# First batch's attention in plain float32 matmuls instead of split float32r operands

## The chip, the cores and the metric

One Trainium2 chip, one core. The metric is the device time of one launch in microseconds (us). The kernel before takes 722.84 us, the median of 3 runs (721.26 to 723.34).

## The reference, cut to what matters

```python
def _attn_ref(q, k, v, M_prev, z_prev, beta):        # B, H, S, D = 4, 8, 576, 64
    scores = (1 / sqrt(D)) * q @ k^T                  # per batch and head, causal
    a = exp(scores - max); a /= a.sum(-1) + 1e-9
    local = a @ v
    q_p = phi(q)                                      # phi(x) = x + 1 if x > 0, else exp(x)
    mem_out = (q_p @ M_prev) / (q_p . z_prev + 1e-6)
    g = 1 / (1 + exp(-beta))                          # per head
    return g * mem_out + (1 - g) * local

def reference(...):
    x = attn_out.transpose(0, 2, 1, 3).reshape(B * S, H * D)     # 2304 x 512
    r = maximum(x @ w_in, 0)                                     # 2304 x 2048
    return (s * r * r + b) @ w_out                               # 2304 x 512
```

All inputs but `w_in` and `w_out` are float32; these two come in as 64-bit floats and are converted on the chip.

## The kernel before, in words

TensorE multiplies float32r operands in one pass, and float32r keeps fewer bits than float32. So the kernel writes a float32 operand as two float32r parts, H (the rounded value) and L (the value less H), and sums the products H·H, H·L and L·H.

The work goes by pairs of heads: pair g holds heads x = 2g and 2g + 1, a batch has NP = 4 pairs, and the first batch is pairs 0 to 3, heads 0 to 7. There are 32 heads. For each of them:

- `load_qk` (L158) loads q and k of a pair, transposed (128 partitions, 64 for each head). `split_qk` (L214) makes parts in the tile `sqk`: H of both by one ACT copy (L223), L of q on one of DVE and POOL and L of k on the other (L220). `stack_qk` (L241) copies these parts by two DMAs a head into `X` (L251), so that one contraction over 128 partitions holds two of the three products.
- `s_mm` (L273) makes the scores of a query tile into PSUM by two matmuls (L278, L279), at least 192 columns wide; the causal tiles have 64, 192, 448, 320 and twice 288 columns. `s_red` (L292, DVE) adds the mask and finds the row's extreme, `s_exp` (L300, ACT) makes P, `s_norm` (L312) scales it on POOL, one tile of the five on DVE.
- `pt_bank` (L335) transposes P block by block on TensorE (L342) into one of five PSUM banks `tps`, and `evac` takes a bank out: ACT writes H (L209), DVE writes L (L213). k block 0 goes to `pt`, the others to `pth` and `ptl`.
- phi(q) is made by ACT, DVE and POOL (L189 to L205), transposed (`t_phi`, L237), taken out as H and L by `evac`, and stacked by two DMAs a head into `Q` (`stack_qp`, L260). `split_v` makes H of M_prev and V on ACT (L269) and L on POOL (L270).
- `av_mm` (L364) sums phi(q)·M and P·V in one PSUM bank `ops`, once for query columns 320 to 575 ("hi", 10 matmuls) and once for columns 0 to 319 ("lo", 6 matmuls), lines L371 to L375; `av_evac` adds the two halves of the output's partitions (ACT copy L387, DVE add L388). There is one bank `ops`, so the next sum waits until the bank is taken out.
- `x_split` makes H and L of the pair's attention output on POOL (L399, L400).

Beside it `split_w` converts w_in in 16 pieces (`conv64`, ACT L78, DVE L79 to L81, POOL L418 and L419). `mm1` (L430 to L432) multiplies the attention output by w_in; its first matmul needs all four pairs of the first batch. `mm1` of batch b runs in between the attention of batch b + 1. From L540 on stands the second stage, the product with w_out, which the change does not touch.

What sets the order: the table `T` at the top gives each task of a head a position (head number plus an offset); the tasks are issued in order of position, and a scheduler in the compiler then orders each engine's instructions by its own model of them. Every engine, and the DMA queue of SP too, works its list in order. The program is one long list without loops.

Of the kernel before, what the change touches and what calls it, by code (L numbers as in the profile page):

```python
# [8 lines left out]
F32 = mybir.dt.float32  # L9
# [18 lines left out]
def attention_moe_kernel(  # L28
# [15 lines left out]
    nc = tc.nc  # L44
# [54 lines left out]
    PTS = []  # L99
    for i in range(2):  # L100
        PTS.append((
            ap1.tile([128, S], F32R, name=f"pt0_{i}"),
            ap1.tile([128, 6, 256], F32R, name=f"pth_{i}"),
            ap1.tile([128, 6, 256], F32R, name=f"ptl_{i}"),
        ))
# [223 lines left out]
    ]}  # L329
    ROW = {(1, 3): 0, (2, 3): 1, (3, 3): 2, (1, 1): 3, (1, 4): 0, (2, 4): 1, (3, 4): 2, (4, 4): 5, (1, 2): 3, (2, 2): 4}  # L330

    def pt_bank(x, blocks):
        P = st["P", x]
        pt0, pth, ptl = PTS[x % 2]
        ps = ps_t.tile([128, 512], F32, tag="t", name="tps")  # L335
        o = 0
        runs = []
        for j, i in blocks:
            kn = 128 if j else 64
            qn = 128 if i else 64  # L340
# [160 lines left out]
    def at(t, fn, *a):  # L501
        EV.append((t, len(EV), fn, a))
# [7 lines left out]
    for n, job in enumerate(JOBS):  # L510
        if job is None:
            continue
        k = len(job[1])
        for i in range(3):
            at(2 * n + TKP[k][i], split_qk, n, i)
        at(2 * n + LQK[k], load_qk, n)
        at(2 * n + LQK[k] + 0.01, load_z, n)
        at(2 * n + LV[k], load_v, n)
# [3 lines left out]
            at(2 * n + PHI[4 + c], t_phi, n, c)  # L522
        for j in range(2):
            x = 2 * n + j
            at(x + SXP[k], stack_qk, x)
            a = [(0,), (1,), (2,), (3,), (4, 0, 288), (4, 288, 288)]
            for pos, a in zip(SP[k], a if k == 5 else a[:3] if k == 3 else a[3:]):
                at(x + pos, t_score, x, *a)
            at(x + SQP[k], stack_qp, x)
            at(x + SPV[k], split_v, x)  # L530
            for pos, bl in zip(PTP[k], PTB[k]):
                at(x + pos, pt_bank, x, bl)
            for c in range(2):
                if CT[c][0] in job[1]:
                    at(x + AVP[k][1 - c], t_av, x, c)
# [268 lines left out]
```

## Time and profile before, and how to read it

| | us |
|---|---|
| median of 3 runs | 722.84 |
| the profiled execution's own time | 729.97 |
| span of that execution, first to last instruction | 727.2 |
| PE busy, share of the span | 630.5, 87% |
| DVE busy | 515.3, 71% |
| ACT busy | 475.2, 65% |
| POOL busy | 459.1, 63% |
| mean granted clock of TensorE | 0.943 |

PE is TensorE's matmuls, PEld its weight loads, DVE the vector engine, ACT the scalar engine, POOL GpSimd, SP the engine that issues the DMAs. Busy time of PE holds the overlapped ends of pipelined matmuls, so what a matmul costs in a row of others is the distance from one start to the next. The granted clock is a mean over a stretch in which the clock stands at one of two levels, 2.4 GHz (1.00) or 1.2 GHz (0.50). The first batch's attention fills about the first 140 us.

### The profile page before, as it was taken

How to read it: one execution, taken by the hardware profiler on the slowest of the kernel's cores; microseconds unless marked ns; L12 is line 12 of the kernel's file. 1: busy time of each engine (PE TensorE's matmuls, PEld its weight loads, DVE VectorE, ACT ScalarE, POOL GpSimd, SP SyncE). 2: the span in 40 equal slices, each digit the busy share in tenths (PEclk: the TensorE clock that was granted, in tenths of full speed). 3: DMA queues.
4: the chain of work that ended last, by engine and by line, in shares of the span. 5: the costliest groups of instructions: out<-in, count | busy, mean ns of one | idle time of the engine just before them, and what ended most of it. 6: DMA issues, size and time to landing. Idle time of an engine off the chain costs nothing. (4 is left out here: it accounts for less than half of the span.)

```text
span 727.2 us, 13086 instructions
## 1 busy us (share of the span) xinstructions
PE 630.5 (87%) x4504; PEld 595.3 (82%) x4504; DVE 515.3 (71%) x1099; ACT 475.2 (65%) x1062; POOL 459.1 (63%) x454
## 2 busy tenths in 40 slices
PE   0667676889889899999999999967869999999997
PEld 0456555789778899999999899967859999999997
DVE  2767798786777766775675753499977867776774
ACT  2556577547667576776776664448878877777851
POOL 4648669756586554655574622488987776565683
PEclk9989988689999899999999999988979999999999
DMA  7968856848788566867786632748355353353301
GB/s 196 280 166 202 208 141 171 208 121 214 182 210 229 149 160 176 218 161 208 207 215 159 161 103 82 265 149 280 134 159 145 117 145 118 115 145 112 102 21 58
DMA packets 73858, 119.87 MB, mean 165 GB/s; under 512 B 10048, under 2 KB 48960, under 8 KB 73792
## 3 DMA queue, kind: packets, MB, share of 16 engines
q1 hardware_dynamic: 73792, 119.04, 59.8%
q8 instruction: 35, 0.57, 0.3%
q14 instruction: 31, 0.25, 0.1%
HBM read 57.68 MB, written 23.59 MB: 112 GB/s over the span
## 5 line engine op out<-in xcount | busy, mean ns | idle before, releaser
L300 ACT ACTIVATE P<-P,mn 128x64 f32<-128x64 f32 (+4 forms) x160 | 89.6, 562 | 42.5 <-DVE mn L292 42.1
L671 PE MATMUL yps<-bH,op 128*128 128x256 f32 x360 | 103.1, 288 | 7.6 <-POOL op L661 6.2
L312 POOL TENSOR_SCALAR P<-P,sm,omg 128x64 f32<-128x64 f32 (+3 forms) x128 | 86.2, 687 | 33.8 <-DVE sm L308 16.3
L669 PE MATMUL yps<-bH,op 128*128 128x256 f32 x360 | 102.9, 286 | 2.4 <-ACT op L660 2.2
L278 PE MATMUL sps<-X 128*128 128x192 f32 (+2 forms) x192 | 69.6, 364 | 40.1 <-DMA X<-sqk 20.7
L670 PE MATMUL yps<-bL,op 128*128 128x256 f32 x360 | 102.5, 285 | 0.0
L342 PE MATMUL tps<-ident,P 128*128 128x128 f32 (+2 forms) x480 | 83.0, 293 | 13.2 <-POOL P L312 5.0
L430 PE MATMUL hps<-xs,w1H 128*128 128x320 f32 (+1 forms) x256 | 80.9, 316 | 10.9 <-ACT r L439 7.8
L430 PE MATMUL hps<-xs,w0H 128*128 128x320 f32 (+1 forms) x256 | 79.0, 312 | 8.1 <-ACT r L439 7.7
L292 DVE CUSTOM_DVE_ANT_0 P<-sps,mask 128x64 f32<-128x64 f32 (+4 forms) x160 | 65.5, 424 | 28.2 <-PE sps L279 24.5
L278 PEld LDWEIGHTS sps<-X 128*128 128x128 f32 x192 | 40.2, 209 | 48.8 <-DVE mn L292 26.0
L342 PEld LDWEIGHTS tps<-ident,P 128*128 128x128 f32 (+2 forms) x480 | 60.4, 142 | 23.4 <-issue 10.4
L431 PE MATMUL hps<-xs,w1H 128*128 128x320 f32 (+1 forms) x256 | 78.3, 306 | 0.0
L432 PE MATMUL hps<-xs,w1L 128*128 128x320 f32 (+1 forms) x256 | 77.6, 305 | 0.0
L671 PEld LDWEIGHTS yps<-bH,op 128*128 128x128 f32 x360 | 69.1, 192 | 9.7 <-POOL op L661 6.4
L432 PE MATMUL hps<-xs,w0L 128*128 128x320 f32 (+1 forms) x256 | 76.9, 302 | 0.0
L431 PE MATMUL hps<-xs,w0H 128*128 128x320 f32 (+1 forms) x256 | 76.8, 301 | 0.0
L669 PEld LDWEIGHTS yps<-bH,op 128*128 128x128 f32 x360 | 69.4, 193 | 3.0 <-ACT op L660 3.0
L439 ACT ACTIVATE r<-hps 128x320 f32<-128x320 f32 (+1 forms) x128 | 49.5, 407 | 31.9 <-PE hps L432 24.7
L670 PEld LDWEIGHTS yps<-bL,op 128*128 128x128 f32 x360 | 69.4, 193 | 0.0
L213 DVE TENSOR_TENSOR ptl<-tps,pth 128x512 fp32r<-128x512 f32 (+1 forms) x96 | 56.5, 595 | 16.6 <-ACT pth L209 10.7
L279 PE MATMUL sps<-X 128*128 128x192 f32 (+2 forms) x192 | 62.4, 327 | 0.0
(119 smaller groups left out, 2052.4 us busy)
## 6 DMA issues: line engine op xcount, KB each, us to landing
X<-sqk SPq DMA_DIRECT2D x64, 432.0 KB, 5.7
r_d<-r SPq DMA_DIRECT2D x32, 320.0 KB, 4.3
qks<-in_qk_t_dram SPq DMA_DIRECT2D x16, 576.0 KB, 5.2
Q<-sqp SPq DMA_DIRECT2D x64, 144.0 KB, 4.5
xa<-in_moe_w_in_dram SPq DMA_DIRECT2D x16, 512.0 KB, 6.4
r_d<-r SPq DMA_DIRECT2D x32, 256.0 KB, 4.3
raw<-in_moe_w_out_dram SPq DMA_DIRECT2D x16, 512.0 KB, 5.6
w1L<-r_d SPq DMA_DIRECT2D x16, 512.0 KB, 4.6
```

Of the source, the lines that this page charges most:

```text
L278: nc.tensor.matmul(ps[:, :m], lhsT=lhsT, rhs=X[:, 1, c0:c0 + m], start=True, stop=False)
L279: nc.tensor.matmul(ps[:, :m], lhsT=lhsT, rhs=X[:, 2, c0:c0 + m], start=False, stop=True)
L292: nc.vector.tensor_tensor_reduce(P[:, PO[i] + c0:PO[i] + c0 + n], ps[:, :n], mask[:, mo:mo + n], -SCALE, init, ALU.add, ALU.min, mn[:, o:o ...
L300: nc.scalar.activation(pt, pt, AF.Exp, scale=-1.0, bias=mn[:, o:o + 1], accum_out=sm[:, i:i + 1])
L312: dve("nm", x // 2, i).tensor_scalar(pt, pt, sm[:, i:i + 1], omg[:, h:h + 1], ALU.mult, ALU.mult)
L342: nc.tensor.transpose(ps[0:kn, o:o + qn], P[0:qn, c:c + kn], ident[0:qn, 0:qn])
L430: nc.tensor.matmul(ps, lhsT=wH[:, p, fs], rhs=xs[:, 0], start=p == 0, stop=False)
L431: nc.tensor.matmul(ps, lhsT=wH[:, p, fs], rhs=xs[:, 1], start=False, stop=False)
L432: nc.tensor.matmul(ps, lhsT=wL[:, p, fs], rhs=xs[:, 0], start=False, stop=p == NP - 1)
L669: nc.tensor.matmul(ps, lhsT=H, rhs=BH, start=f == 0, stop=False)
L670: nc.tensor.matmul(ps, lhsT=H, rhs=BL, start=False, stop=False)
L671: nc.tensor.matmul(ps, lhsT=L, rhs=BH, start=False, stop=f == KF - 1)
```

## The change

For heads 0 to 7 q, k, phi(q), M, V and P^T stay float32, and TensorE gets them as float32. q and k are loaded straight into their place (`sqk` for pairs 0 and 1, the memory of `X` for pairs 2 and 3), M and V into `V`; `split_qk`, `stack_qk`, `stack_qp` and `split_v` are not issued for these pairs. A score tile is one matmul over a head's 64 partitions, without the minimum of 192 columns. `t_phi` and `pt_bank` take a bank out by one ACT copy. `av_mm32` makes 64 output partitions by 6 ("hi") and 4 ("lo") matmuls, leaving out columns whose P is zero, and one DVE copy takes them out. The fills of `pth` and `ptl` with zeros move from the start to heads 8 and 9. Pairs 4 to 15 and the table `T` are as before.

```diff
+    def new_pts(i, dtype):
+        PTS[i] = pts = tuple(ap1.tile(s, dtype, tag=f"{n}_{i}", name=f"{n}_{i}")
+                             for n, s in (("pt0", [128, S]), ("pth", [128, 6, 256]), ("ptl", [128, 6, 256])))
+        if dtype == F32R:
+            for t in pts[1:]:
+                nc.gpsimd.memset(t[:, 4:6, 0:128].bitcast(F32), 0.0)
...
@@ load_qk
-        st["qk", g] = t = ap1.tile([128, 2, S], F32, tag="qks", name="qks")
+        if g < NP:
+            if g < 2:
+                t = qk[:, 2 * g:2 * g + 2].bitcast(F32)
+            else:
+                t = ap1.tile([128, 2, S], F32, tag=f"X{g % 2}", name="qk32")
...
@@ load_v
+        if g < NP:
+            st["V", 2 * g] = st["V", 2 * g + 1] = t = ap2.tile([128, 6, 2, D], F32, tag="V", name="V32")
...
@@ t_phi
+        if g < NP:
+            nc.scalar.copy(s[:, cs], ps[:, :o])
+        else:
+            evac(s[:, 0, cs], s[:, 1, cs], ps[:, :o], ("phl", g, c))
...
@@ s_mm
+        if x < 2 * NP:
+            t = st["qk", x // 2][64 * (x % 2):64 * (x % 2) + 64]
+            nc.tensor.matmul(ps[:, :n], lhsT=t[:, 0, QS[i]:QS[i] + 128], rhs=t[:, 1, c0:c0 + n], start=True, stop=True)
+            return ps
...
+    def pt_evac(x, H_out, L_out, ps, key):
+        if x < 2 * NP:
+            nc.scalar.copy(H_out, ps)
+        else:
+            evac(H_out, L_out, ps, key)
...
+    def av_mm32(x, hi):
+        g, j = divmod(x, 2)
+        V, Q = st["V", x], st["sqp", g]
+        pt0, pth, _ = PTS[j]
+        ps = ps_o.tile([128, 512], F32, tag="o", name="ops")
+        q0, n = CO[hi], CW[hi]
+        rs = slice(64 * j, 64 * j + 64)
+        off = 0 if hi else 64
+        nc.tensor.matmul(ps[0:64, :n], lhsT=V[rs, 0, j], rhs=Q[rs, q0:q0 + n], start=True, stop=False)
+        nc.tensor.matmul(ps[0:64, :n], lhsT=V[rs, 1, j], rhs=pt0[rs, q0:q0 + n], start=False, stop=False)
+        for r, c, o in ((0, 2, 0), (1, 3, 0), (2, 4, 0), (5, 5, 128)) if hi else ((3, 2, 0), (4, 3, 128)):
+            nc.tensor.matmul(ps[0:64, off + o:n], lhsT=V[:, c, j], rhs=pth[:, r, o:], start=False, stop=r in (4, 5))
+        return ps
...
@@ av_evac
+        if x < 2 * NP:
+            nc.vector.tensor_copy(xo[ma, :], ps[0:64, :n])
+            return
...
@@ the list of tasks
+        own = n >= NP
         for i in range(3):
-            at(2 * n + TKP[k][i], split_qk, n, i)
+            if own:
+                at(2 * n + TKP[k][i], split_qk, n, i)
...
-            at(x + SXP[k], stack_qk, x)
+            if own:
+                at(x + SXP[k], stack_qk, x)
...
-            at(x + SQP[k], stack_qp, x)
-            at(x + SPV[k], split_v, x)
+            if own:
+                at(x + SQP[k], stack_qp, x)
+                at(x + SPV[k], split_v, x)
```

How the order moves, at three places. First the DMA queue of SP at the start. Before, from its sixth entry on (`qks` are q and k of a pair, `X_146` and `X_174` the stacks of heads 0 and 1, `xa` pieces of w_in):

```order
L177 DMA qs<-in_q_rows_dram 128x640
L183 DMA vs<-in_vm_dram 128x768
L251 DMA X_146<-sqk 64x1728
L163 DMA qks<-in_qk_t_dram 128x1152
L251 DMA X_146<-sqk 64x3x576
L251 DMA X_174<-sqk 64x3x576
L251 DMA X_174<-sqk 64x1728
L183 DMA vs<-in_vm_dram 128x768
L171 DMA z<-in_z_prev_dram 128x128
L406 DMA xa<-in_moe_w_in_dram 128x1024 x3
```

Now, from the same entry:

```order
L183 DMA qs<-in_q_rows_dram 128x640
L169 DMA sqk<-in_qk_t_dram 128x1152
L192 DMA V_152<-in_vm_dram 128x768
L169 DMA qk_194<-in_qk_t_dram 128x1152
L192 DMA V_284<-in_vm_dram 128x768
L169 DMA qk_375<-in_qk_t_dram 128x1152
L169 DMA qks<-in_qk_t_dram 128x1152
L192 DMA vs<-in_vm_dram 128x768
L177 DMA z<-in_z_prev_dram 128x128
L455 DMA xa<-in_moe_w_in_dram 128x1024 x3
```

The stacks are gone; the loads of pairs 1 to 4 stand ahead of the first pieces of w_in.

Second, DVE about head 1's way out (a row that only reads an accumulator is shown once). Before (`x_398` is pair 0's output, `pth` and `ptl` the parts of P^T, here of head 2):

```order
L388 TENSOR_TENSOR x_398<-ops,xc 64x320
L312 TENSOR_SCALAR P<-P,sm,omg 128x320
L213 TENSOR_TENSOR ptl_104<-tps,pth_103 128x4x128 x2
L213 TENSOR_TENSOR ptl_104<-tps,pth_103 128x2x128
L213 TENSOR_TENSOR pt_0_102<-tps,pt_0_102 64x64
L292 ISA P,mn<-sps,mask 128x64
L292 ISA mn 128x1
L292 ISA P,mn<-sps,mask 128x192
L220 TENSOR_TENSOR sqk<-qks,sqk 128x576
L213 TENSOR_TENSOR pt_0_102<-tps,pt_0_102 64x512
L292 ISA P,mn<-sps,mask 128x448
```

Now (`x_326` is pair 0's output):

```order
L432 COPY x_326<-ops 64x320
L311 ISA P,mn<-sps,mask 128x448
L311 ISA mn 128x1
L311 ISA P,mn<-sps,mask 128x320
L311 ISA P,mn<-sps,mask 128x288
L229 TENSOR_TENSOR sqk<-qks,sqk 128x576
L311 ISA P,mn<-sps,mask,mn 128x288
L311 ISA P,mn<-sps,mask 128x64
L311 ISA P,mn<-sps,mask 128x192
L326 TENSOR_SCALAR sm<-sm 128x5
L327 RECIPROCAL sm<-sm 128x5
```

The subtractions for the parts L are gone; reductions of scores follow each other. The one `sqk` entry that is left belongs to pair 4.

Third, PE about the "hi" sum of head 4. Before (`X_850` is the stack of head 7, `pth_103` and `ptl_104` the parts of P^T of head 4):

```order
L372 MATMUL ops<-pt_0_102,V 128x256
L374 MATMUL ops<-pth_103,V 128x256
L375 MATMUL ops<-ptl_104,V 128x256
L278 MATMUL sps<-X_850 128x192
L279 MATMUL sps<-X_850 128x192
L278 MATMUL sps<-X_850 128x448
L279 MATMUL sps<-X_850 128x448
```

Now (`qk_375` is q and k of pair 3 in float32, here for head 6, `V_472` M and V of pair 2):

```order
L292 MATMUL sps<-qk_375 128x320
L403 MATMUL ops<-pt_0_229,V_472 64x256
L405 MATMUL ops<-pth_230,V_472 64x256 x3
L405 MATMUL ops<-pth_230,V_472 64x128
L292 MATMUL sps<-qk_375 128x288 x2
```

Each pair of float32r matmuls over parts has become one float32 matmul; the first matmul of `mm1` still follows the sums of head 7, as before.

## Rows read from the trace of the kernel before

**Rows 1.** Busy time of each engine, granted clock and DMA share in stretches of the span: columns are the stretch, its length, PE, PEld, DVE, ACT and POOL busy (instructions), PEclk, DMA share, GB/s. The first matmul of the scores starts at 17.15, the first transposes of P at 30.30, the first matmul of `mm1` at 140.5.

```profile
17.10:30.30 13.20, 9.57 (x29) 7.08 (x29) 8.71 (x34) 8.64 (x24) 5.49 (x6) 1.00 1.03 294
30.30:140.50 110.20, 75.37 (x385) 61.35 (x385) 87.64 (x233) 66.83 (x176) 77.27 (x85) 0.83 0.74 187
140.50:160.00 19.50, 16.14 (x98) 15.53 (x98) 15.09 (x32) 11.24 (x30) 11.79 (x14) 0.82 0.42 113
160.00:200.00 40.00, 36.39 (x268) 34.65 (x267) 29.18 (x81) 25.93 (x71) 24.71 (x27) 0.96 0.82 202
250.00:450.00 200.00, 197.74 (x1481) 188.35 (x1480) 130.86 (x385) 138.71 (x377) 102.66 (x126) 1.00 0.65 170
```

**Rows 2.** The timeline of the start, and the first matmul of `mm1`: start, length, engine, line, operation, tiles, count, and in brackets the idle time before it and what ended it.

```profile
0.74 0.40 SPq L163 DMA_DIRECT2D qks<-in_qk_t_dram  x1
4.35 1.15 ACT L223 CAST sqk<-qks 128x1152 fp32r<-128x1152 f32 x1 [2.11 <-DMA qks<-in_qk_t_dram]
...
9.22 0.74 ACT L189 ACTIVATE phr<-qs 128x640 f32<-128x640 f32 x1 [2.30 <-DMA qs<-in_q_rows_dram]
9.98 0.74 ACT L190 ACTIVATE qs<-qs 128x640 f32<-128x640 f32 x1
10.75 0.82 DVE L194 SCALAR_TENSOR_TENSOR qs<-qs,phr 128x640 f32<-128x640 f32 x1 [2.74 <-ACT qs L190]
14.18 1.53 POOL L195 TENSOR_TENSOR phr<-qs,z 128x640 f32<-128x640 f32 x1
15.74 0.82 DVE L201 TENSOR_REDUCE nrm<-phr 128x10 f32<-128x640 f32 x1 [4.17 <-POOL phr L195]
17.15 0.53 PE L278 MATMUL sps<-X 128*128 128x192 f32 x1 [17.15 <-DMA X<-sqk]
18.43 1.26 POOL L205 TENSOR_TENSOR qs<-qs,nrm 128x640 f32<-128x640 f32 x1 [2.72 <-DVE nrm L204]
...
24.70 0.67 ACT L78 ACTIVATE w<-xa 128x512 f32<-128x512 f32 x1
28.05 3.00 POOL L312 TENSOR_SCALAR P<-P,sm,omg 128x64 f32<-128x64 f32 x4 [2.98 <-DVE sm L308]
30.30 1.12 PE L342 MATMUL tps<-ident,P 128*128 128x128 f32 x4 [1.08 <-POOL P L312]
...
140.46 0.42 PE L430 MATMUL hps<-xs,w0H 128*128 128x320 f32 x1
```

**Rows 3.** What PE waited for between 30.3 and 140.5: engine, line, what it waited for, us in total, times, longest.

```profile
PE sps L278 <- DVE mn L292: 12.5, 14, 3.6
PE ops L371 <- DVE x L388: 4.5, 5, 1.9
PE tps L342 <- DVE ptl L213: 4.1, 3, 3.1
PE tps L342 <- DVE pt L213: 4.0, 1, 4.0
PE sps L278 <- DMA X<-sqk: 3.5, 1, 3.5
PE tps L342 <- POOL P L312: 2.8, 3, 1.1
PE tps L237 <- POOL qs L205: 2.4, 1, 2.4
```

**Rows 4.** Groups of instructions between 30.3 and 140.5 that the change takes away or replaces: line, engine, operation, tiles, count, busy us, mean ns, idle before.

```profile
L213 DVE TENSOR_TENSOR ptl<-tps,pth 128x512 fp32r<-128x512 f32 (+1 forms) x25 | 14.9, 598 | 2.9 <-ACT pth L209 2.6 <-ACT pt L209 0.2
L213 DVE TENSOR_TENSOR pt<-tps,pt 64x64 fp32r<-64x64 f32 (+1 forms) x16 | 7.0, 449 | 0.3
L213 DVE TENSOR_TENSOR sqp<-tps,sqp 128x320 fp32r<-128x320 f32 x4 | 1.9, 482 | 3.8 <-ACT sqp L209 3.8
L213 DVE TENSOR_TENSOR sqp<-tps,sqp 128x256 fp32r<-128x256 f32 x4 | 1.7, 415 | 0.0
L220 DVE TENSOR_TENSOR sqk<-qks,sqk 128x576 fp32r<-128x576 f32 x4 | 3.4, 853 | 8.1 <-ACT sqk L223 8.1
L388 DVE TENSOR_TENSOR x<-ops,xc 64x256 f32<-64x256 f32 (+1 forms) x16 | 7.2, 451 | 1.9 <-ACT xc L387 1.7
L387 ACT COPY xc<-ops 64x256 f32<-64x256 f32 (+1 forms) x16 | 6.3, 391 | 5.9 <-PE ops L375 5.5
L223 ACT CAST sqk<-qks 128x1152 fp32r<-128x1152 f32 x4 | 4.6, 1153 | 10.1 <-POOL P L312 4.2 <-DMA z<-in_z_prev_dram 2.9 <-POOL w0H L418 2.9
L269 ACT CAST V<-vs 128x384 fp32r<-128x384 f32 x8 | 4.1, 510 | 1.3 <-DMA vs<-in_vm_dram 1.2
L270 POOL TENSOR_TENSOR V<-vs,V 128x384 fp32r<-128x384 f32 x7 | 9.4, 1349 | 8.5 <-ACT V L269 8.5
L220 POOL TENSOR_TENSOR sqk<-qks,sqk 128x576 fp32r<-128x576 f32 x4 | 7.8, 1948 | 8.4 <-ACT sqk L223 8.4
```

**Rows 5.** The timeline of PE just ahead of `mm1`, and about 300 us, where the granted clock is 1.00 and PE does not wait; the distance of the starts is what a matmul costs there. Columns as in Rows 2.

```profile
139.20 0.71 PE L342 MATMUL tps<-ident,P 128*128 128x128 f32 x4
139.75 0.38 PE L237 MATMUL tps<-ident,qs 128*128 128x128 f32 x2
...
299.80 0.28 PE L430 MATMUL hps<-xs,w0H 128*128 128x256 f32 x1
299.92 0.28 PE L431 MATMUL hps<-xs,w0H 128*128 128x256 f32 x1
300.04 0.28 PE L432 MATMUL hps<-xs,w0L 128*128 128x256 f32 x1
...
300.42 0.60 PE L342 MATMUL tps<-ident,P 128*64 128x128 f32 x4
300.78 0.39 PE L371 MATMUL ops<-Q,V 128*128 128x320 f32 x1
```

**Rows 6.** As Rows 1, in two stretches of 20 us of the first batch.

```profile
80.00:100.00 20.00, 13.75 (x69) 11.64 (x70) 14.94 (x42) 11.58 (x30) 17.26 (x20) 0.74 0.61 165
120.00:140.00 20.00, 15.65 (x74) 13.31 (x75) 17.19 (x45) 10.38 (x30) 13.52 (x16) 0.66 0.83 207
```

**Rows 7.** DMAs that fill `X`, over the whole span (page, part 6): KB each, median us from issue to landing.

```profile
X<-sqk SPq DMA_DIRECT2D x64, 432.0 KB, 5.7
```

More of the change, by code (lines that the diff above doesn't have):

```diff
@@ L98, in attention_moe_kernel @@
     mask = ap1.tile([128, 448], F32, name="mask")
[L99 to L105, printed above, removed]
+    PTS = [None, None]
+    def new_pts(i, dtype):
[4 more added lines that the diff above has]
+                nc.gpsimd.memset(t[:, 4:6, 0:128].bitcast(F32), 0.0)
     qk = ap1.tile([128, 4, S], F32R, name="sqk")
@@ L116, in setup @@
         )
-        for pt0, pth, ptl in PTS:
-            for t in (pth, ptl):
-                nc.gpsimd.memset(t[:, 4:6, 0:128].bitcast(F32), 0.0)
         braw = gin
@@ L160, in load_qk @@
         b, p, _, _, qc, kc = parts(g)
-        st["qk", g] = t = ap1.tile([128, 2, S], F32, tag="qks", name="qks")
+        if g < NP:
[3 more added lines that the diff above has]
+                t = ap1.tile([128, 2, S], F32, tag=f"X{g % 2}", name="qk32")
+            st["qk", g] = t
+        else:
+            st["qk", g] = t = ap1.tile([128, 2, S], F32, tag="qks", name="qks")
         for n, c in ((slice(0, 2), kc),) if qc == kc else ((slice(0, 1), qc), (slice(1, 2), kc)):
@@ L181, in load_v @@
         b, p, _, kt, _, _ = parts(g)
-        st["v", g] = t = ap1.tile([128, 6, 2, D], F32, tag="vs", name="vs")[:, :kt.stop + 1]
+        if g < NP:
+            st["V", 2 * g] = st["V", 2 * g + 1] = t = ap2.tile([128, 6, 2, D], F32, tag="V", name="V32")
+        else:
+            st["v", g] = t = ap1.tile([128, 6, 2, D], F32, tag="vs", name="vs")[:, :kt.stop + 1]
         nc.sync.dma_start(t, vm[b, p][:, :kt.stop + 1])
@@ L228, in t_phi @@
     def t_phi(g, c):
-        if ("sqp", g) not in st:
+        if g < NP:
+            if c == 0:
+                st["sqp", g] = ap1.tile([128, S], F32, tag=f"Q{g % 2}", name="sqp32")
+        elif ("sqp", g) not in st:
             st["sqp", g] = ap1.tile([128, 2, S], F32R, tag="sqp", name="sqp")
@@ L239, in t_phi @@
         cs = slice(CO[c], CO[c] + CW[c])
-        evac(s[:, 0, cs], s[:, 1, cs], ps[:, :o], ("phl", g, c))
+        if g < NP:
+            nc.scalar.copy(s[:, cs], ps[:, :o])
+        else:
+            evac(s[:, 0, cs], s[:, 1, cs], ps[:, :o], ("phl", g, c))
     def stack_qk(x):
@@ L273, in s_mm @@
     def s_mm(x, i, c0, n):
+        ps = ps_s.tile([128, 512], F32, tag="s", name="sps")
+        if x < 2 * NP:
+            t = st["qk", x // 2][64 * (x % 2):64 * (x % 2) + 64]
+            nc.tensor.matmul(ps[:, :n], lhsT=t[:, 0, QS[i]:QS[i] + 128], rhs=t[:, 1, c0:c0 + n], start=True, stop=True)
+            return ps
         X = st["X", x]
-        ps = ps_s.tile([128, 512], F32, tag="s", name="sps")
         m = max(n, 192)
@@ L330, in attention_moe_kernel @@
     ROW = {(1, 3): 0, (2, 3): 1, (3, 3): 2, (1, 1): 3, (1, 4): 0, (2, 4): 1, (3, 4): 2, (4, 4): 5, (1, 2): 3, (2, 2): 4}
+    def pt_evac(x, H_out, L_out, ps, key):
+        if x < 2 * NP:
+            nc.scalar.copy(H_out, ps)
+        else:
+            evac(H_out, L_out, ps, key)
     def pt_bank(x, blocks):
         P = st["P", x]
+        if x // 2 in (0, NP) and ("pts", x) not in st:
+            st["pts", x] = True
+            new_pts(x % 2, F32R if x // 2 else F32)
         pt0, pth, ptl = PTS[x % 2]
@@ L356, in pt_bank @@
             if kind == "k0":
-                evac(pt0[0:64, a:a + n], pt0[64:128, a:a + n], ps[0:64, o:o + n], ("ptl", x, id(blocks), kind, a))
+                h0 = 64 * (x % 2) if x < 2 * NP else 0
+                pt_evac(x, pt0[h0:h0 + 64, a:a + n], pt0[64:128, a:a + n], ps[0:64, o:o + n], ("ptl", x, id(blocks), kind, a))
             else:
                 cs = slice(128 * kind, 128 * kind + 128)
-                evac(pth[:, a:a + n, cs], ptl[:, a:a + n, cs],
+                pt_evac(x, pth[:, a:a + n, cs], ptl[:, a:a + n, cs],
                      ps[:, o:o + 128 * n].rearrange("p (r c) -> p r c", c=128), ("ptl", x, id(blocks), kind, a))
+    def av_mm32(x, hi):
[11 more added lines that the diff above has]
+        return ps
     def av_mm(x, hi):
+        if x < 2 * NP:
+            return av_mm32(x, hi)
         V, Q = st["V", x], st["Q", x]
@@ L383, in av_evac @@
         xo = st["x", g, hi]
+        ma = slice(64 * j, 64 * j + 64)
+        if x < 2 * NP:
+            nc.vector.tensor_copy(xo[ma, :], ps[0:64, :n])
+            return
         xc = ap1.tile([128, 320], F32, tag="xc", name="xc")
-        ma = slice(64 * j, 64 * j + 64)
         co = slice(64 - 64 * j, 128 - 64 * j)
```

## The prediction

> **What bounds the kernel now.** I read the busy table by stretches first. From 250 to 450 us PE is busy 197.7 of 200 us at a granted clock of 1.00 [rows 1]: there TensorE sets the pace, and nothing of it changes. The first batch is another stage. `mm1` cannot start before all four pairs are done, and starts at 140.46 [rows 2]. Between the first transposes of P at 30.30 and this point lie 110.2 us, in which DVE is busy 87.6, POOL 77.3, PE 75.4 and ACT 66.8 [rows 1]. No engine is full, DVE comes nearest (80%). PE's waits there are mostly for DVE: 12.5 us for score reductions, 8.1 for subtractions that make L of P^T, 4.5 for the output's add; 3.5 us go to the DMA that stacks X [rows 3]. So the first batch is bound by DVE and by chains through it.
>
> The start is a chain of its own: q and k have landed at 4.35, but the first score matmul starts at 17.15 since casting, subtracting and stacking lie between; P of head 0 is scaled by POOL from 28.05, and the transposes start at 30.30 [rows 2].
>
> The end of the kernel moves as the start of `mm1` moves, as long as the later lists are the same, which the order of PE bears out: the same matmuls follow the sums of head 7.
>
> **The change part by part: the start.** The first scores can start when q and k have landed, at 4.35 [rows 2]. What comes last then is phi, whose transposes PE's list still has ahead of those of P, and on POOL the scaling of P behind it. From the rows: phi's inputs at 9.22, 0.74 and 0.74 on ACT with an exponential of some 0.5 between, 0.82 on DVE, 1.53 on POOL, 0.82 on DVE and some 0.4 for two small operations, 1.26 on POOL [rows 2], some 0.6 for reductions ahead on DVE: 16.6; then three of the four pieces of P's scaling, 3.00 x 3/4 = 2.2 us [rows 2]: about 19, against 30.3, a gain of 11. One thing takes a little of it back: ACT's list has the first conversion of w_in ahead of the first copy of P^T, and on SP's queue this piece of w_in now stands behind the loads of pairs 1 to 4. It started at 24.70 before [rows 2], and I let it cost 1 us. **Gain 10 us.**
>
> **DVE, ACT and POOL in the 110.2 us.** DVE loses L of P^T, 14.9 + 7.0 us, of which 0.7 stays with head 8 (one of 25 in the first group has been done by then), L of phi for pairs 1 to 3, three quarters of 1.9 + 1.7 = 2.7, and L of q or k for two of four pairs, 1.7 [rows 4]: together 25.6, so 62.0 are left. The add of 451 ns that takes `ops` out becomes a copy of the same size, counted as 0; it reads one operand for two, and its bounds are 0 and half of 7.2 us, on an engine that no longer binds. ACT loses xc, 6.3, three quarters of V's casts, 3.1, and half of q and k's, 2.3 [rows 4]: 55 left; its copies for casts cost the same. POOL loses six of seven V parts, 8.1, and half of 7.8, 3.9 [rows 4], and gains four fills that stood at the start: 65 left. On SP's queue eight heads lose four DMAs each, of which the ones into X took 5.7 us to land [rows 7]. The load of M and V of pair 2 now waits on this queue until the sums of pair 0 are done, and the loads of q behind it wait too; it is needed one and a half heads later, more than 10 us, which covers a load of such a length. I count it as 0; without that cover it would cost up to 5.7 us.
>
> **PE.** Here the change adds. At a clock of 1.00 a float32r matmul of 256 columns costs 0.12 us from start to start, 0.47 ns a column [rows 5]. A head's scores take 2 x 1,728 columns now, 1.6 us, its sums 4,224, 2.0 us. After the change a head has 1,600 columns of scores and 2,432 of sums (1,408 "hi", 1,024 "lo"), in float32. Within this stretch the scores of heads 2 to 7 and the sums of eight heads are float32: 6 x 1,600 + 8 x 2,432 = 29,056 columns. No row shows a float32 product. The nearest rows are transposes, which are float32 too: 128 columns cost 0.09 us about 300 us [rows 5], 0.70 ns a column; that makes 20.4 us and is the lower bound. The upper bound: two operands of two halves make four products of halves, so four float32r passes, 4 x 0.47 = 1.88 ns a column, 54.6 us. I take the upper one. A transpose only moves values, while a float32 product has to keep what the kernel now sums from three products.
>
> The Trainium skill says for this that true float32 makes four passes through the array ("FP8 and Floating Point Precision", section TensorE Precision Notes); by the transposes' rows the sum for PE would be 41 us, by that rule 75. No run here shows it yet.
>
> To this come scores of heads 8, 9 and a part of 10 as before, 2 x 1.6 + 0.4 = 3.6, and 156 transposes at some 0.11 us (0.09 about 300 us, 0.55 / 4 = 0.14 ahead of `mm1` [rows 5]), 17.2. Sum 75.4 us at full clock, where it is 46 now. PE becomes the longest engine.
>
> **The clock.** In this stretch it was granted at 0.83 on average [rows 1], with 0.66 in one part and 0.74 in another [rows 6], a mixture of both levels (1.2 and 2.4 GHz). Where PE worked more, it was higher: 0.96 with 36.4 of 40 us busy, 1.00 with 197.7 of 200 [rows 1]. With PE as the longest engine I take 0.90: 75.4 / 0.90 = 83.8. Waits that remain: of PE's 34.8 idle us the subtractions' 8.1 and the stack's 3.5 go, and as DVE falls from 88 to 62 I keep a third of its 17.0; with POOL's 5.2 this makes some 12 [rows 1, 3]. **The stretch: 96 us for 110.2, a gain of 14.**
>
> **Sum.** 10 + 14 = 24 us. The profiled execution took 729.97 itself (span 727.2), so 706 by its time; its median of runs is 722.84, 1.0% lower, and 24 us off that gives **699 us**.
>
> **The rivals.**
>
> *Float32 products are cheap.* If they cost as the transposes' rows, PE has 41 us and POOL with 65 is longest. The stretch is 110.2 for 87.6 busy us of the longest engine now, 1.26; at that ratio 65 x 1.26 = 82, a gain of 28 + 10: 685 us. For it: the only float32 rows there are. Against it: transposes multiply nothing.
>
> *The waits stay.* The positions in the table were made for the kernel before, and PE, ACT and SP work in order. If PE idles for all that is not directly removed, 34.8 - 11.6 = 23 us, the stretch is 107 and the time 710 us.
>
> *Slower: PE at the low level.* PE's 75.4 us are a price at 2.4 GHz. If the clock stays as low as in the worst part now or lower, because matmuls of 64 partitions or 64 outputs do not raise it, PE's list alone takes the stretch. The point where this decides: 75.4 / c + 12 = 110.2 + 10 gives c = 0.70. Now 0.66 and 0.74 occur in parts, 0.83 on average. At 0.60 the stretch is 138, 28 more than now; less the start's 10 this gives 741 us. For it: clock falls are there already; against it: a PE that hardly waits has been granted 0.96 and more [rows 1].
>
> **How the numbers follow.** Chances: forecast 0.48, cheap products 0.22, waits stay 0.15, nothing gained because one takes the other 0.03, slower 0.12. A measurement of this kernel tells about 0.3%, 2.2 us, from no change. Faster by more than that: 0.48 + 0.22 + 0.12 of the third = 0.82; within: 0.03 + 0.03 = 0.06; slower 0.12. The range: below, cheap products and shorter waits together (65 x 1.17 = 76, start 10: a gain of 44) give 679; above, the third rival with a part of the clock's fall, up to no gain, 722. What lies beyond is the slower case and little of the lower one.
>
> **What would show it.** The first score matmul at about 4.5 us; the first transposes of P at 19 to 21 us; `mm1` starting at about 116 us; float32 matmuls of 256 columns some 0.48 us apart at full clock (0.18 would be the first rival); the granted clock between these points near 0.9; DVE busy some 62 us there. PE's waits for subtractions of P^T gone, waits for score reductions down to a few us. The prediction is wrong if PE is busy all through the stretch at a clock under 0.70, if a float32 matmul costs clearly more than four passes, or if `mm1` starts at 116 and the end does not follow, because PE then waits for w_in's conversions.

## The result, and the profile after

| | before | after |
|---|---|---|
| median, us (4 runs each) | 723.09 (721.26 to 723.39) | 711.28 (707.91 to 713.85) |
| ratio, 95% interval | | 0.984 (0.981 to 0.988) |
| the profiled execution's own time | 729.97 | 707.91 |
| first score matmul | 17.15 | 4.27 |
| first transposes of P | 30.30 | 20.47 |
| first matmul of `mm1` | 140.46 | 130.42 |
| from the transposes to `mm1` | 110.2 | 110.0 |

Ratios and their intervals are taken over the fast runs of both kernels, so they can differ a little from the quotient of the medians shown. The change gained 11.8 us by the medians. All of it that can be placed is the start: `mm1` begins 10.0 us earlier. The stretch from the first transposes to `mm1`, for which a gain of 14 us was forecast, is as long as it was. (Behind `mm1`'s start the two profiled executions differ by 11.0 us more, 586.7 against 575.7; the one of before was itself 6.9 us above its median, so most of this is not the change.)

Busy time by stretch, the columns as in [rows 1], which the first, second and last line answer; the two of 20 us answer [rows 6]:

```profile
4.27:20.47 16.20, 12.50 (x27) 6.32 (x27) 7.68 (x30) 7.84 (x24) 5.33 (x6) 1.00 0.84 328
20.47:130.42 109.95, 92.88 (x421) 54.85 (x420) 69.84 (x193) 59.05 (x155) 71.30 (x84) 0.97 0.44 113
...
60.00:80.00 20.00, 19.61 (x94) 11.19 (x93) 13.34 (x44) 12.91 (x36) 13.00 (x16) 1.00 0.33 99
80.00:100.00 20.00, 19.75 (x94) 11.06 (x92) 12.03 (x39) 12.36 (x35) 13.80 (x16) 1.00 0.33 84
...
240.00:440.00 200.00, 198.87 (x1501) 190.59 (x1500) 128.18 (x374) 135.87 (x367) 105.05 (x129) 1.00 0.63 168
```

In the stretch PE rose from 75.4 to 92.9 busy us, DVE fell from 87.6 to 69.8 and ACT from 66.8 to 59.1. PE is now the longest engine, and from 60 to 100 us it is full. Behind the stretch nothing has become a new bound: the steady part is as before.

What PE waited for from 20.47 to 130.42, columns as in [rows 3]; these four are all of its waits there:

```profile
PE tps L249 <- POOL qs L214: 8.7, 1, 8.7
PE ops L402 <- DVE x L432: 3.5, 6, 1.2
PE sps L297 <- DMA X<-sqk: 2.5, 1, 2.5
PE sps L297 <- DVE mn L311: 2.2, 2, 1.1
```

The waits for the subtractions of P^T (8.1 us in [rows 3]) are gone, and 12.5 us for score reductions have become 2.2. In their place stands one single wait of 8.7 us, for phi(q) of pair 1 (L214 writes it, L249 transposes it). Where it comes from is read from the timelines of SP, PE, ACT, DVE and POOL around it (five fences, one an engine, columns as in [rows 2]):

```profile
3.58 0.43 SPq L183 DMA_DIRECT2D qs<-in_q_rows_dram  x1
...
19.35 0.33 SPq L183 DMA_DIRECT2D qs<-in_q_rows_dram  x1
```

```profile
18.17 1.11 PE L249 MATMUL tps<-ident,qs 128*128 128x128 f32 x4
19.22 1.32 PE L292 MATMUL sps<-sqk 64*128 64x288 f32 x2
20.47 1.11 PE L370 MATMUL tps<-ident,P 128*128 128x128 f32 x4
21.52 1.33 PE L292 MATMUL sps<-sqk 64*128 64x288 f32 x2
22.77 1.11 PE L402 MATMUL ops<-sqp,V 64*64 64x256 f32 x2
23.81 1.43 PE L292 MATMUL sps<-sqk 64*128 64x64 f32 x4
33.98 0.98 PE L249 MATMUL tps<-ident,qs 64*128 64x64 f32 x3 [8.74 <-POOL qs L214]
34.76 1.06 PE L370 MATMUL tps<-ident,P 128*128 128x128 f32 x4
35.61 0.64 PE L249 MATMUL tps<-ident,qs 128*128 128x128 f32 x2
36.04 3.63 PE L370 MATMUL tps<-ident,P 128*128 128x128 f32 x22
39.60 0.64 PE L403 MATMUL ops<-pt,V 64*64 64x256 f32 x2
40.17 1.73 PE L405 MATMUL ops<-pth,V 128*64 128x256 f32 x8
41.83 1.55 PE L292 MATMUL sps<-sqk 64*128 64x448 f32 x4
```

```profile
24.71 0.72 ACT L198 ACTIVATE phr<-qs 128x640 f32<-128x640 f32 x1
```

```profile
26.72 0.82 DVE L203 SCALAR_TENSOR_TENSOR qs<-qs,phr 128x640 f32<-128x640 f32 x1
```

```profile
26.50 3.19 POOL L331 TENSOR_SCALAR P<-P,sm,omg 128x64 f32<-128x64 f32 x4 [0.43 <-DVE sm L327]
29.66 1.53 POOL L204 TENSOR_TENSOR phr<-qs,z 128x640 f32<-128x640 f32 x1
32.67 1.26 POOL L214 TENSOR_TENSOR qs<-qs,nrm 128x640 f32<-128x640 f32 x1 [1.48 <-DVE nrm L213]
```

There is one buffer `qs`. Pair 0's phi is held in it until its transposes at 18.17 to 19.2, so the q of pair 1 is loaded at 19.35, 15.8 us behind that of pair 0. From there its phi takes its way through ACT, DVE and POOL, where it stands behind the scaling of head 1's P, and is done at 33.9. PE's list has the transposes of this phi ahead of those of head 1's P, and PE stands still from 25.2 to 34.0. In the kernel before, the same wait was 2.4 us [rows 3]: there PE reached these transposes later, at 38.77.

The price of the new matmuls is read from the PE rows above. Each float32 matmul leaves two records, and its price is the distance to the next group's start: 1.66 us for the 8 records at 40.17 (four matmuls, 3 x 256 + 128 = 896 columns), 1.85 ns a column; 0.57 us for one of 256 columns at 39.60, 2.2 ns. A float32r matmul cost 0.47 ns a column [rows 5].

Two groups of the stretch that answer to [rows 4], columns as there, and below them the DMA issues that answer to [rows 7]:

```profile
L432 DVE COPY x<-ops 64x256 f32<-64x256 f32 (+1 forms) x16 | 7.2, 448 | 12.9 <-PE ops L405 12.8
...
L222 DVE TENSOR_TENSOR ptl<-tps,pth 128x512 fp32r<-128x512 f32 x2 | 1.4, 692 | 3.7 <-ACT pth L218 3.7
```

```profile
X<-sqk SPq DMA_DIRECT2D x48, 432.0 KB, 5.5
```

The copy that takes `ops` out costs 448 ns where the add cost 451, as taken. DVE now waits 12.8 us for PE at these copies: the roles are exchanged. Of the 25 subtractions for `ptl` two are left, of the 64 stacking DMAs 48.

### The profile page after: what moved, and what is told of

It is laid out like the page before. It is cut to its first block, busy times and chain, and to the rows that moved or that the text cites. A ratio compares the mean times of both kernels' runs of the same rounds, so it can differ in the third digit from the quotient of the medians.

```text
span 706.1 us, 12939 instructions
## 1 busy us (share of the span) xinstructions
PE 646.3 (92%) x4536; PEld 584.5 (83%) x4536; DVE 487.2 (69%) x1047; ACT 462.4 (65%) x1034; POOL 443.8 (63%) x442
## 4 chain that ended last, share of the span: by engine, by line
PE 60%; DMA 11%; DVE 11%; ACT 7%; issue 5%; POOL 5%; SPq 0%; ACTq 0%; DVEq 0%; POOLq 0%
PE yps L724 7%; PE yps L722 6%; PE yps L723 6%; PE hps L479 6%; PE tps L370 6%; PE hps L480 6%; PE hps L481 6%; DMA X<-sqk 5%; PE sps L292 2%; PE sps L297 2%; PE sps L298 2%; PE ops L420 2%; PE ops L421 2%; PE ops L405 2%; DMA qs<-in_q_rows_dram 2%
## 5 line engine op out<-in xcount | busy, mean ns | idle before, releaser
L331 POOL TENSOR_SCALAR P<-P,sm,omg 128x64 f32<-128x64 f32 (+3 forms) x128 | 88.2, 701 | 32.6 <-DVE sm L327 15.4
L479 PE MATMUL hps<-xs,w1H 128*128 128x320 f32 (+1 forms) x256 | 81.0, 316 | 11.8 <-ACT r L488 9.3
L370 PE MATMUL tps<-ident,P 128*128 128x128 f32 (+2 forms) x480 | 78.5, 282 | 0.9 <-POOL P L331 0.8
L480 PE MATMUL hps<-xs,w1H 128*128 128x320 f32 (+1 forms) x256 | 78.1, 305 | 0.0
L722 PEld LDWEIGHTS yps<-bH,op 128*128 128x128 f32 x360 | 69.8, 194 | 1.7 <-ACT op L713 1.7
L723 PEld LDWEIGHTS yps<-bL,op 128*128 128x128 f32 x360 | 69.8, 194 | 0.0
L370 PEld LDWEIGHTS tps<-ident,P 128*128 128x128 f32 (+2 forms) x480 | 56.9, 136 | 12.5 <-issue 7.5
L479 PEld LDWEIGHTS hps<-xs,w1H 128*128 128x128 f32 x256 | 50.6, 198 | 13.8 <-ACT r L488 10.2
L479 PEld LDWEIGHTS hps<-xs,w0H 128*128 128x128 f32 x256 | 49.1, 193 | 10.3 <-ACT r L488 8.3
L222 DVE TENSOR_TENSOR ptl<-tps,pth 128x512 fp32r<-128x512 f32 (+1 forms) x72 | 42.4, 595 | 16.0 <-ACT pth L218 10.9
L297 PE MATMUL sps<-X 128*128 128x192 f32 (+1 forms) x144 | 47.1, 330 | 6.0 <-DVE mn L311 3.3
```

Source lines behind the costliest of these rows:

```text
L331: dve("nm", x // 2, i).tensor_scalar(pt, pt, sm[:, i:i + 1], omg[:, h:h + 1], ALU.mult, ALU.mult)
L479: nc.tensor.matmul(ps, lhsT=wH[:, p, fs], rhs=xs[:, 0], start=p == 0, stop=False)
L480: nc.tensor.matmul(ps, lhsT=wH[:, p, fs], rhs=xs[:, 1], start=False, stop=False)
L722: nc.tensor.matmul(ps, lhsT=H, rhs=BH, start=f == 0, stop=False)
L723: nc.tensor.matmul(ps, lhsT=H, rhs=BL, start=False, stop=False)
```

## The experiments

Ratios are to the kernel before on the same chip in the same set; its medians in the three sets were 728.34 (first four kernels below), 729.87 (next four) and 725.37 (last four), so kernels are compared by ratio. P is the first transposes of P, M the first matmul of `mm1`; busy time and granted clock are those of the stretch between.

| kernel | median, us | ratio (95%) | P | M | PE / DVE busy | clock |
|---|---|---|---|---|---|---|
| the change | 711.28 | 0.984 (0.981 to 0.988) | 20.5 | 130.4 | 92.9 / 69.8 | 0.97 |
| pair1 | 722.11 | 0.995 (0.992 to 0.999) | 22.2 | 138.4 | 77.7 / 83.7 | 0.88 |
| pair2 | 711.94 | 0.982 (0.978 to 0.986) | 20.7 | 131.4 | 84.9 / 81.0 | 0.88 |
| onepass | 700.84 | 0.966 (0.961 to 0.971) | 22.7 | 126.8 | 65.3 / 67.5 | 0.72 |
| q1early | 703.45 | 0.968 (0.963 to 0.974) | 19.7 | 123.7 | 98.2 / 68.6 | 0.93 |
| q1one | 693.81 | 0.952 (0.948 to 0.956) | 23.2 | 117.8 | 67.5 / 65.2 | 0.71 |
| q1pair1 | 710.92 | 0.976 (0.971 to 0.981) | 20.5 | 127.5 | 76.8 / 83.7 | 0.90 |
| q1pair2 | 702.79 | 0.965 (0.961 to 0.969) | 20.0 | 132.1 | 92.1 / 82.7 | 0.88 |
| q1av1 | 711.94 | 0.976 (0.971 to 0.981) | 20.6 | 129.7 | 91.2 / 70.1 | 0.92 |
| again | 710.07 | 0.980 (0.976 to 0.984) | 21.3 | 128.9 | 92.2 / 67.8 | 0.98 |
| bq1 | 726.48 | 1.003 (0.999 to 1.006) | 34.8 | 145.1 | 78.1 / 89.9 | 0.75 |
| q12 | 702.80 | 0.968 (0.964 to 0.973) | | | | |
| q12pair2 | 710.46 | 0.974 (0.966 to 0.981) | 20.0 | 136.0 | 91.8 / 86.6 | 0.82 |

Some things limit what the table tells. P, M, busy time and clock are of one execution each: `again` is the changed kernel a second time, and its M is 1.6 us earlier. From M to the end these executions took 571 to 587 us, so M alone does not give the time. And the scheduler made new lists for every edit: DVE's list of onepass differs from the change's from its second entry on, PE's list of q1early from about the first transposes of P. A difference holds the edit together with the order that came of it. The clock column counts the start too high; the last section shows by how much.

### How many pairs: pair1 and pair2

The pairs in plain float32 are counted by a constant of its own, 1 or 2 in place of 4; the other pairs go by parts and stacks as before. The last float32 pair has its q and k in the memory of the stack `X1`, so this stack is free only after that pair's scores.

```diff
+    N32 = 1        # pair2: 2
-        if g < NP:
+        if g < N32:
...
-        own = n >= NP
+        own = n >= N32
```

> Only pair 0 (heads 0 and 1) in plain float32, pairs 1 to 3 by parts as in the kernel before. Theory A (the whole gain of the change is its earlier start, about 10 us, and in the rest of the first batch the float32 matmuls put on TensorE what they take from DVE): first transposes of P near 20 us, mm1 at 128 to 131 us, time about 711, no slower than the change. Theory B (the gain comes evenly from all eight heads, by DVE's relief): a quarter of the change's 12 us, about 720.

> Pairs 0 and 1 in plain float32, pairs 2 and 3 by parts. Theory A: start as with the change, then two pairs at TensorE's price and two at DVE's; about 708 to 712. Theory B: half of 12 us, about 717.

Measured: one pair gives almost nothing (0.995), two pairs give all of it (0.982). So the start's gain does not come through by itself. With one pair PE's longest waits in the stretch are these:

```profile
PE tps L250 <- POOL qs L215: 12.8, 3, 9.6
PE sps L298 <- DVE mn L312: 11.3, 10, 3.5
```

The wait for phi is there as well, 12.8 us, and behind it the heads that are still split keep DVE at 83.7 busy us. The 8.1 us won at the start (transposes of P at 22.2 and not 30.3) are for the most part lost again before `mm1`, which starts 2.1 us earlier than in the kernel before. Pairs 2 and 3 in float32 change nothing (0.982 against 0.984 and 0.980): they take 11 us off DVE and put 8 on PE.

### What the passes cost: onepass

The float32 matmuls of the change read the upper halves of their operands as bfloat16, so the kernel leaves out what the lower halves add.

```diff
-lhsT=V[:, c, j], rhs=pth[:, r, o:]
+lhsT=V[:, c, j].bitcast(BF16).rearrange("p (n two) -> p n two", two=2)[:, :, 1], rhs=pth[:, r, o:]...
```

> The changed kernel, but the float32 matmuls of heads 0 to 7 read only the upper 16 bits of each float32 operand as bfloat16, one pass in place of four; copies, loads and order else as in the change (part of the computation is left out). Theory A (TensorE's price of float32 binds the first batch): some 45 of 61 us of TensorE's time go, then POOL (65 us) and DVE (62 us) with waits bind, so the stretch from the first transposes to mm1 falls from 110 to about 85 us and the time to about 688. Theory C (waits and the order of the lists bind, TensorE is only busy beside them): within 3 us of the change, 708 to 714.

Measured 700.84, 0.966: some 1.4% to 1.8% better than the change, between the two theories' times (688, and 708 to 714). PE's busy time fell by 27.6 us, but the stretch by only 5.9. The first line is the stretch, the second the piece from 40 to 60 us (columns as in [rows 1]); then PE's longest waits:

```profile
22.74:126.79 104.05, 65.28 (x301) 41.28 (x300) 67.46 (x185) 58.13 (x154) 64.01 (x77) 0.72 0.44 118
...
40.00:60.00 20.00, 9.77 (x41) 4.94 (x41) 14.83 (x38) 9.04 (x25) 13.78 (x17) 0.63 0.31 98
```

```profile
PE tps L250 <- POOL qs L215: 15.6, 3, 8.6
PE ops L403 <- DVE x L433: 8.7, 8, 1.8
PE tps L371 <- POOL P L332: 4.9, 1, 4.9
PE sps L293 <- DVE mn L312: 4.8, 6, 1.3
```

Idle time grew from 17 to 39 us, above all for phi again, and the granted clock fell from 0.97 to 0.72. So the four passes are not the only thing that holds the stretch. How much of it is the new order of the lists is not shown: the first transposes of P came 2.3 us later here, at 22.74.

### The wait for phi: q1early

The q of pair 1 goes into a buffer of its own (the one that `split_v` needs only from pair 4 on), so that its load doesn't wait for pair 0.

```diff
-        st["q", g] = t = ap1.tile([128, 5, 2, D], F32, tag="qs", name="qs")
+        st["q", g] = t = ap1.tile([128, 5, 2, D], F32, tag="vs" if g == 1 else "qs", name="qs")
```

> The changed kernel with a buffer of its own for q of pair 1 (phi's input), so that its load does not wait until phi of pair 0 is transposed. Theory A: TensorE's wait of 8.7 us at 25 to 34 us goes and TensorE, full from there on, passes the gain to the end: mm1 at 121 to 124 us, time about 703. Theory D (the wait only moves, since DVE, ACT or POOL are no further): mm1 at 128 to 131 us, time 709 to 712.

Measured 703.45, 0.968, as the theory of the late q had it. The load is issued at 4.53 and the wait is down to 1.1 us. The timeline of SP, that of PE, and then busy time in the stretch and in two pieces of it (columns as in [rows 1]):

```profile
4.53 0.43 SPq L183 DMA_DIRECT2D qs<-in_q_rows_dram  x1
```

```profile
26.57 0.98 PE L249 MATMUL tps<-ident,qs 64*128 64x64 f32 x3 [1.11 <-POOL qs L214]
27.34 1.06 PE L370 MATMUL tps<-ident,P 128*128 128x128 f32 x4
```

```profile
19.72:123.68 103.96, 98.17 (x421) 55.67 (x422) 68.58 (x188) 57.88 (x154) 67.55 (x80) 0.93 0.43 118
...
40.00:45.00 5.00, 5.00 (x12) 1.93 (x11) 1.38 (x6) 0.87 (x2) 1.61 (x2) 0.50 0.35 105
45.00:50.00 5.00, 5.00 (x13) 2.55 (x13) 1.77 (x7) 0.99 (x4) 2.43 (x4) 0.50 0.00 0
```

The phi transposes come 7.4 us earlier, `mm1` 6.7 us. PE is now busy 98.2 of 104.0 us: the stretch is PE's list. Most of its rise from 92.9 is the clock: between 40 and 50 us it stood at 0.50 although PE had no idle time, and counted at full clock (an estimate, made as in the section on the prediction) PE's work is 86 us here and 85 in the change.

### Both together: q1one

q1early with the one pass of onepass (both edits above).

> The changed kernel with both edits: q of pair 1 in a buffer of its own, and one bfloat16 pass over the upper halves in place of each float32 matmul of heads 0 to 7 (part of the computation is left out). After the wait for phi is gone TensorE is busy 98 of 104 us before mm1. Theory A (from there on TensorE's price of float32 is the limit): without it mm1 starts at 105 to 113 us and the time is 686 to 694. Theory E (another chain, phi's or P's, stands right behind it at the same length): mm1 at 120 to 124 us, time 698 to 704.

Measured 693.81, 0.952 (0.948 to 0.956): 1.65% under q1early, 12 us by the ratios and 9.6 by the medians, which come from two sets. That is what the passes beyond the first cost once the wait is gone, with the new order that came with them.

```profile
23.19:117.84 94.65, 67.51 (x301) 41.32 (x300) 65.21 (x183) 55.87 (x149) 65.68 (x80) 0.71 0.50 135
```

PE has 30.7 busy us less than in q1early and 21.4 more idle ones: no engine is full any more (POOL 65.7, DVE 65.2 of 94.7), and at a clock of 0.71 PE's own work costs more. `mm1` started later than expected, the time was as expected.

### Fewer pairs without the wait: q1pair1 and q1pair2

pair1 and pair2 with q1early's line.

> Only pair 0 in plain float32, as in the run of that kind before, with q of pair 1 in a buffer of its own. There the transposes of P came 8 us earlier and TensorE then waited 12.8 us for phi. Theory F (the start's gain is handed on once phi of pair 1 is not late): mm1 at 128 to 131 us, time 710 to 714. Theory G (behind it DVE with the parts of P^T binds): mm1 at 136 to 139, time 718 to 721.

> Pairs 0 and 1 in plain float32, q of pair 1 in a buffer of its own. TensorE was busy 85 us of 111 before mm1 and waited 10.0 us for phi. Theory F: these 10 us go to the end, mm1 at 121 to 123 us, time 702 to 705, the same as with all four pairs. Theory G (DVE, 81 of 111 us busy, binds): mm1 at 127 to 131, time 708 to 712.

Measured 0.976 and 0.965, both the times expected if the start's gain is handed on as soon as phi of pair 1 is early. For one pair the early q is worth 1.9% (0.995 to 0.976), for two 1.7%, for four 1.2% to 1.6%. With it, one pair in float32 already brings 2.4%, the second 1.1% more, the third and fourth nothing (0.965 against 0.968, intervals overlapping). In q1pair2 `mm1` starts only at 132.1, where 121 to 123 was expected with this time and 127 to 131 with the rival's, and yet the time is the lowest of the kernels with four passes. PE has no more matmuls ahead of `mm1` than in pair2 (404 records against 403), but they take 92.1 busy us and not 84.9. The profiled execution was the longest of its six, 707.41 against a median of 702.79. So theory F is borne out by the time and not by `mm1`; where the time is won back behind it is not shown.

### Scores by parts, sums in float32: q1av1

q1early, but the scores of pairs 1 to 3 by parts and stacks as before.

```diff
+    NS = 1
-        if x < 2 * NP:        # s_mm, load_qk
+        if x < 2 * NS:
...
-            if own:           # split_qk, stack_qk
+            if n >= NS:
```

> q of pair 1 in a buffer of its own; the sums of all eight heads in plain float32, but the scores of pairs 1 to 3 by parts with the stacks in X. Against the kernel with q's buffer alone TensorE loses some 7 to 12 us of 98, POOL gains 6, ACT 3.5, DVE 2.5 us and the DMAs of 12 stacks come back. Theory A: mm1 at 114 to 120 us, time 694 to 700. Theory H (the stacks' DMA chain costs what TensorE gains): mm1 at 122 to 128, time 702 to 708.

Measured 0.976, 0.8% above q1early and more than any theory gave (its profiled execution, 715.55, was the longest of six). PE saved 7 busy us and waited instead:

```profile
PE sps L298 <- DMA X<-sqk: 6.9, 2, 3.9
PE sps L298 <- DVE P L332: 3.9, 1, 3.9
```

So the float32 scores are worth their passes: what they save is less DVE's time (70.1 against 68.6) than the stacking DMAs' landing. The second wait belongs to them too: DVE's scaling of P ended at 30.6, a stack landed at 31.03, and PE went on at 31.12.

### The change once more, the early q alone, and more buffers: again, bq1, q12, q12pair2

`again` is the change as it is. `bq1` is the kernel before with a second place for the q of pair 1, `q12` the change with such places for pairs 1 and 2, `q12pair2` the same with pairs 0 and 1 alone in float32.

```diff
-        st["q", g] = t = ap1.tile([128, 5, 2, D], F32, tag="qs", name="qs")
+        st["q", g] = t = rpool.tile([128, 5, 2, D], F32, tag="r", name="qs") if g in (1,) else ap1.tile(...)   # q12: (1, 2)
```

> The changed kernel once more, on the chip of the three kernels that it is compared with. If the first timing holds: 1.6% faster than the kernel before, ratio 0.981 to 0.988. Its variants with an early phi of pair 1 had 0.968 and 0.965; if that was the chip and not the edit, its ratio here is near theirs, 0.965 to 0.972.

> The kernel before with q of pair 1 in a buffer of its own, nothing else. Theory F (the late phi is a wait that only the change's earlier start lays open; before, TensorE waited 2.4 us for phi): within 3 us of the kernel before. Rival (an early phi helps whatever the start): 6 to 10 us faster than the kernel before.

> The changed kernel with buffers of their own for q of pairs 1 and 2. With pair 1 alone TensorE was busy 98 of 104 us before mm1 and waited 1.1 us for phi: theory A, TensorE's float32 price is the limit then, so pair 2 adds at most 2 us: ratio 0.964 to 0.972. Rival (phi is late for every pair, hidden in the busy time): ratio 0.955 to 0.962.

> Pairs 0 and 1 in plain float32, pairs 2 and 3 by parts, q of pairs 1 and 2 in buffers of their own. With pair 1's alone 0.965, the same as with all four pairs in float32. Theory A (the last two pairs cost TensorE what they save DVE): again within 0.5% of the kernel with four pairs and both buffers. Rival: one of them is more than 5 us ahead.

Measured in one set: the change 0.980, q12 0.968, so the early q is worth 1.2% (7.3 us by the medians) beside the change, and pair 2's adds nothing to pair 1's. bq1 gives 1.003 (0.999 to 1.006): in the kernel before the early q brings no gain. It isn't a clean test, since the added load delays the first stacks (its first score matmul starts at 20.80, not 17.15, the first transposes of P at 34.78); but from there to `mm1` it takes 110.3 us, as before, although PE's wait for this phi is gone. q12pair2 missed: expected like q12, it gave 0.974, by the medians 7.7 us behind q12 as its rival had it, but with an interval of 0.966 to 0.981, too wide to tell.

## Why the prediction was wrong in size

**Right: the start.** First scores at 4.27 (about 4.5 forecast), first transposes of P at 20.47 (19 to 21), a gain of 9.8 us against 10. The chain was right up to its last step: phi was done at 16.5 (16.6 forecast), and POOL scaled P from 16.97 to 19.50. The last us is luck. It was put down to a conversion of w_in on ACT, but ACT had done with this at 20.7 and waited 0.9 us for the transposes; what PE did until 20.47 was a score matmul of head 1.

**Right: what a float32 matmul costs.** Four float32r passes, 1.88 ns a column, were taken, and the rows show 1.85 to 2.2 at full clock, 2.0 on average in the stretch. The Trainium skill's rule that true float32 makes four passes ("FP8 and Floating Point Precision", section TensorE Precision Notes) agrees with these rows. The rival of cheap products is excluded.

**Right: who binds.** PE became the longest engine, the subtractions' waits went, the waits for reductions fell. DVE fell less than forecast, to 69.8 and not 62: eight conversions of w_in and not seven lie in the stretch, and its small operations were slower. That it cost much is not seen: PE waits 5.7 us for DVE in the stretch.

**Wrong: "The stretch: 96 us for 110.2, a gain of 14."** It took 110.0. Both terms failed:

- *The waits, 12 us forecast, 17.1 measured.* The waits were taken from those of before, less what the change removes. A wait that the change lengthens was not among them: the 2.4 us for phi of pair 1 became 8.7. The chain of phi was followed for pair 0, where it sets the start; that pair 1's load hangs on the same single buffer, and so could not come earlier by as much as PE does, was not asked. The delay looked for on SP's queue was another one, at pair 2's M and V, counted as 0. q1early shows the cause: that one line, with the order the scheduler made of it, is worth 1.2% to 1.6%, q12 shows the same with another buffer in another set, and with it the kernel is 3.2% under before, 23 us of 723, which is about the 24 us of the forecast.
- *PE's busy time, 83.8 us forecast, 92.9 measured.* Summed by the distances of starts, float32 matmuls took 61.4 us (54.6 / 0.90 = 60.7 forecast), transposes 25.2 (19.1), scores by parts 6.1 (4.0). The transposes have the largest share. They cost 0.21 us each until 37.65 and 0.11 behind it, so the 22 at 36.04, which lie across that point, make 3.56 us: up to there PE ran at the low level of its clock, as the last section shows. Counted at full clock (an estimate: the distances of starts, with the time up to 37.65 and the two later stretches at 0.50 taken half) PE's work is 85 us, and 75.4 was forecast: float32 59.3 for 54.6, transposes 20.5 for 17.2, scores by parts 5.4 for 3.6. So it was the list of work that was sized too small, in all three parts. The clock was not: taken so, its mean in the stretch is 0.89, and 0.90 was forecast, though from a column that reads the stretch before as 0.83 where this count gives 0.77.

The agreement of q1early with 699 is no proof of the working: its PE has 98 us of work in 104, not 84 in 96. The passes' price of 10 to 12 us (q1one against q1early) stays in it.

**The rivals.** "The waits stay" gave 710 us and is nearest in time, but it had PE idle for 23 us and busy for 84; PE was idle for 17 and busy for 93. Its reason, positions made for another kernel with engines that work in order, fits the phi wait. The slower case needed a clock under 0.70; it was 0.97 in the stretch by the column, 0.89 counted as above. That the 9.8 us of the start reached the end is due to pairs 0 and 1 together: pair1 lost most of its 8.1 on the way.

**Open.** Whether the early q is worth the most where the fewest pairs are float32 (1.9%, 1.7% and 1.2% to 1.6%, from ratios whose intervals reach about half a per cent to each side), and what q12pair2's spread comes from.

## What to carry to other kernels

When a chain at the start is shortened, go through the loads whose buffer is released inside that chain: their consumers come earlier by the whole gain, and a wait that was covered shows up in front of them. Work moved from DVE and DMA to more passes on TensorE pays while TensorE has idle time; here two pairs of four gave all of it, the other two exchanged one engine's time for the other's. Cutting passes afterwards gives back less than the busy time says, since idle time and a lower clock take most of it.

## What the runs showed of the hardware

The granted clock went with how much PE had to do in passes: 0.97 in the stretch with float32, 0.72 and 0.71 in the two kernels with one pass, where PE idled 27 to 39 us of it. So a smaller list was worked off more slowly: counted at full clock, PE's work fell by 41 us from the change to onepass (85 to 44), its busy time by 27.6. The clock also stood at 0.50 from 40 to 50 us in q1early with PE busy all the time; in the 5 us ahead of that PE had been busy for 3.0:

```profile
35.00:40.00 5.00, 3.01 (x9) 1.66 (x9) 4.33 (x9) 2.07 (x6) 2.80 (x3) 0.82 0.42 121
```

And the clock shown for the start isn't the one that matmuls ran at. Two windows of the change read 1.00 alike (columns as in [rows 1]):

```profile
20.00:25.00 5.00, 5.00 (x14) 2.42 (x12) 2.79 (x8) 3.41 (x7) 0.82 (x2) 1.00 0.37 147
...
40.00:45.00 5.00, 5.00 (x20) 2.46 (x19) 2.54 (x7) 4.76 (x14) 1.52 (x2) 1.00 0.35 110
```

Yet at 22.77 one float32 matmul of 256 columns took 1.04 us to the next start, and at 39.60 it took 0.57: nearly half the speed, as the lower level of 1.2 GHz would give. The reason is that the column counts as 1.00 what has no record: the first record of the clock in this trace begins at 37.65, at 1.00. Transposes of 128 columns, start to start, took 0.21 us up to that point (four from 34.76 to 35.61, in PE's timeline of the section on the result) and 0.11 from it on:

```profile
37.68 0.93 PE L370 MATMUL tps<-ident,P 128*128 128x128 f32 x7
```

In all 13 traces that have such transposes on both sides of their first record (which begins between 31 and 48 us) it is 0.21 ahead of it and 0.11 behind. The Trainium skill ("TensorE: Matmul & The Clock Gate", section "What's actually happening") names this level as the gate's default for an engine that has been idle. The start of the program fits that; but PE was busy without a pause from 14.64 to 25.24 in the change and stayed at it. With the time ahead of the first record counted as 0.50, the mean clock of the stretch is 0.89 and not 0.97 in the change, 0.65 and not 0.72 in onepass, 0.66 and not 0.71 in q1one. About 8.4 us of the change's PE work in the stretch (20.47 to 25.24, 33.98 to 37.65) went at the low level; this belongs to the 0.90 that was forecast, not to the 9 us that PE took beyond the forecast.
